# Four constants of an instruction schedule: an earlier start of attention, more dense work per block of keys, closer requests for weights

## The chip, the core and the metric

The kernel runs on one core of a Trainium2 chip. A core has TensorE (PE in the profile; its weight loads are the separate row PEld), VectorE (DVE), ScalarE (ACT), GpSimd (POOL) and SyncE (SP, which here issues every DMA). The metric is device time in microseconds (us); less is better. The kernel before took 713.68 us, the median of three runs that lie between 712.69 and 714.38 us. One more execution was profiled: it took 713.22 us, and the span from its first to its last instruction is 711.4 us, so 1.8 us lie outside the span.

## The reference, cut to what matters

The input x has 2048 rows of 512 numbers. The output mixes an attention block and an MLP row by row:

```
g = sigmoid((x * gate_w).sum(-1))
q, k, v = split(x @ wqkv)                  # 32 heads of 16
scores = q @ k.T / 4, kept where 0 <= query - key < 256
a = softmax(scores) @ v @ wo
b = gelu_tanh(x @ w1 + b1) @ w2 + b2       # 512 -> 1792 -> 512
out = g * a + (1 - g) * b
```

The kernel makes every dense product in three matmuls (high part times high part, high times low, low times high), so that two rounded factors together keep float32 accuracy.

## The kernel before, in words

**Dense work.** The rows are cut into four tiles of 512. One generator, `dense()` (L946), yields all dense work in pieces of three 128x512 matmuls (`mm3`, L124): first `qkv(t)` for the tiles 0 to 3 (eight q/k products and four v products each), then eight turns of `mlp`, then the output projection `final`. A turn of `mlp` is a tile with one half of the hidden columns: an **u stage** (28 pieces, the first MLP product; its results go through `gelu`, L746, three DVE and four ACT instructions per 128x512 block) and a **y stage** (28 pieces, the second product). There are thus eight u stages; the text numbers them u0 to u7 and the y stages y0 to y7.

**Attention.** Heads are taken four at a time in 8 groups, and the keys of a group in 16 blocks of 128: 128 steps of the loop at L976. A step holds four **maxima** (`att_max`, L539: matmul `sm` on PE, then a row maximum on DVE, L555), which run 12 steps ahead (`LEAD`), four **exponentials** (`att_exp`, L584: matmul `st` on PE, exponential on ACT, L617), and a mask of the block's edges on POOL (L611). After every fourth step `att_pvs` (L623) makes the product with v (`pv_sm` and `pv_st`, 64 to 96 small matmuls), evacuated by ACT (L660) and DVE (L663). After every fourth maximum step `att_rows` (L561) turns the maxima on DVE, and POOL copies them in eight casts into spare rows of `qs` (L577).

**What sets the order.** The program is written by hand, engine by engine: each engine executes its instructions in the order in which the Python code emits them, and waits for semaphores. The code keeps a clock of its own, `now`, in nanoseconds, which sets only the order and no time on the chip; `after(ns, fn)` emits something when that clock has moved on by `ns`. PE's order is written by `fill`, which emits dense pieces (counted at 681 ns each) until a budget is used up:

```
    fill(START - AHEAD)
    for c in (0, 1):
        load_ks(0, c)
    fill(AHEAD)
    for u in range(-LEAD, NU):
        step = STEP if u >= 0 else STEP0
        ... four times: one maximum, one exponential, fill(step / 4)
```

So `START` is the dense work ahead of the first maximum, `STEP0` (2750) the dense work in each of the 12 steps that hold maxima alone, and `STEP` the dense work in each of the 128 full steps. The dense work that the generator holds up to the output projection comes to 436.1 us by the code's count. In the y stages maxima and exponentials stand in pairs, in the u stages singly.

**Loads.** All DMAs go through SP's queue in order. `load_kd`, `load_qd`, `load_ks` and `load_qs` fetch the keys and queries of a group from DRAM. The two `load_ks` above stand `AHEAD` (9 us of dense work) before the first maximum; the first queries, `load_qd(0, 0)` and `load_qd(0, 1)`, are emitted at fixed pieces of `qkv(2)` (L447).

**Weights of the MLP.** `load` (L220) spaces the requests for w1, w2 and wo by at least `PACE` on the code's clock. A request that comes before `RAWS` lands in a spare half of a buffer of the exponentials (`half_pt`), and its low part is later subtracted on POOL (L201); one that comes after `RAWS` lands in one of two buffers `raw`, so that no more than two are under way, and its low part is subtracted on DVE (L201 too). The high part is always a copy on ACT (L197).

Of the kernel before, what the change touches and what calls it, by code (L numbers as in the profile page):

```python
# [32 lines left out]
def gated_mix(ctx: ExitStack, tc: tile.TileContext, x, wqkv, wo, w1, b1, w2, b2, gate_w, out):  # L33
# [100 lines left out]
    def after(ns, fn, *args):  # L134
        now[1] += 1
        heapq.heappush(todo, (now[0] + ns, now[1], fn, args))
# [20 lines left out]
    def half_pt(name):  # L157

        if not spare:
            v = sb.tile([128, 2, 2, 320], F32, tag="pt", bufs=PTS, name=name)  # L160
            v = v.rearrange("p h a b -> p h (a b)")
            spare.extend(v[:, h, 0:T] for h in (1, 0))
        return spare.pop()
# [4 lines left out]
    def load_raw(key, early=False):  # L168
# [6 lines left out]
        if early and kind == "v":  # L175
            if i == 0:
                raws["v"] = f32(sb.tile([128, NC, 2, T], F32R, tag="xt", bufs=1, name="raw_v"))
            raw = raws["v"][:, i, 0]
        elif early or now[0] < RAWS:
            raw = half_pt(f"raw_{kind}{i}")  # L180
# [39 lines left out]
    def load(key):  # L220

        paced[0] = max(now[0], paced[0] + PACE)
        after(paced[0] - now[0], load_now, key)
# [3 lines left out]
    def load_now(key):  # L227
        if now[0] >= RAWS:
            if slots[0] - slots[1] == 2:
                return after(500, load_now, key)  # L230
            slots[0] += 1
            after(LAND, split, key, nc.vector, True)
        else:
            after(LAND + 3000, split, key, nc.gpsimd)
        load_raw(key)
# [723 lines left out]
    def fill(ns):  # L959

        owed[0] += ns
        while owed[0] > 0:
            c = next(run)
            if c is None:
                owed[0] = -1e9
            else:
                owed[0] -= c
                tick(c)

    NU = NG * NKB  # L970
    NQ = NG * NT
# [5 lines that stand above are left out]
        m = u + LEAD  # L977
        gm, bm = divmod(m, NKB)
        step = STEP if u >= 0 else STEP0
        for i in range(4):  # L980
# [46 lines left out]
RB = 4  # L1027
NKB = S // 128
PTS = 7
RAWS = 152000.0  # L1030
PUT = 1200
LEAD = 12
QAT = 5
START = 105000.0
NORM = 6000
YSWAP = 3
GELU = (700, 1500, 3600, 4600, 6000, 7000)
XAT = 3
ORDER = 'mspf'
XOR = 1  # L1040
PACE = 4000.0
LAND = 7500.0
REACH = 2500.0
LAND0 = 11000.0
# [11 lines left out]
HELD = 2  # L1056
YAT = 5
YGAP = 2500
STEP = 2330.0
_TC = dict()  # L1060
_INS = ["A_x", "A_wqkv", "A_wo", "B_w1", "B_b1", "B_w2", "B_b2", "gate_w"]

# [17 lines left out]
```

## Time and profile before

| | |
|---|---|
| median of 3 runs | 713.68 us (712.69 to 714.38) |
| the profiled execution | 713.22 us, span 711.4 us |
| PE, PEld, DVE, ACT, POOL busy | 694.0, 596.5, 511.6, 419.6, 365.2 us |
| qkv(3), up to the first u matmul | ends 142.2 us after the span's start |
| u0 | 142.2 to 174.2 |
| u1 | 207.65 to 239.2 |
| u3 | 335.55 to 368.5 |
| u4 | 401.8 to 435.9 |
| output projection | 660.3 to 711.4 |

A row of the waits names the engine and line that waited, after the arrow who released it, and then the total in us, the number of waits and the longest. PE and PEld are one instruction stream: a weight load that waits holds the matmul behind it. A matmul's end is modelled, so that PE is shown as busy for a while after its last real step; a row of PEld is shown as idle from the end of its last load. A row of the stage table gives the stretch, its length, the busy time of each engine with the number of its instructions, the granted clock, the DMA engines' share and GB/s.

### The profile page before, as it was taken

To read this page: it belongs to the slowest core of one execution; us is meant where nothing else is said; L and a number is where in the kernel's file an instruction comes from. 1 tells how busy PE (TensorE), PEld (TensorE's weight loads), DVE (VectorE), ACT (ScalarE), POOL (GpSimd) and SP (SyncE) were. 2 spreads that over 40 slices of the span, in tenths; PEclk is the share of its full clock that TensorE was granted. 3 is DMA by queue.
4 is the path that set the end of the run, shared out by engine and by line. 5 is a ranking of instruction groups with operands and counts; after the bars stand their busy time and mean duration, and the time that the engine had idled before them with its cause. 6 is when DMAs were issued, how large, how long until landed. Compare 5 with 4: busy or idle time off the path is not lost.

```text
span 711.4 us, 17481 instructions
## 1 busy us (share of the span) xinstructions
PE 694.0 (98%) x6129; PEld 596.5 (84%) x6129; DVE 511.6 (72%) x1561; ACT 419.6 (59%) x972; POOL 365.2 (51%) x852
## 2 busy tenths in 40 slices
PE   9999999998999999999999999999999999999988
PEld 7888888886888888888888877888888888868876
DVE  4632425798769967986898799678968886875552
ACT  4434533378448845864795488458746853885451
POOL 5200001559756866776687578757865875620000
PEclk9999999999999999999999999999999999999999
DMA  9989798999996899999886989997899899477573
GB/s 315 355 256 364 261 373 279 266 295 246 245 249 155 211 274 249 217 279 277 220 194 176 240 234 247 252 260 174 185 246 239 194 260 270 124 217 230 188 243 119
DMA packets 179256, 172.09 MB, mean 242 GB/s; under 512 B 56673, under 2 KB 122977, under 8 KB 179169
## 3 DMA queue, kind: packets, MB, share of 16 engines
q1 hardware_dynamic: 179168, 170.97, 87.4%
q8 instruction: 49, 0.80, 0.5%
q14 instruction: 39, 0.31, 0.2%
HBM read 112.73 MB, written 62.39 MB: 246 GB/s over the span
## 4 chain that ended last, share of the span: by engine, by line
PE 77%; DVE 8%; ACT 5%; DMA 5%; POOL 3%; issue 1%; SPq 0%; DVEq 0%; ACTq 0%; POOLq 0%
PE sm L551 8%; PE pv_sm L639 7%; PE st L595 7%; PE y L127 6%; PE y L129 6%; PE y L128 6%; PE u L127 4%; PE qk L127 4%; PE u L129 4%; PE qk L129 4%; PE u L128 4%; PE qk L128 4%; DVE sm L555 3%; PE v L127 2%; PE v L129 2%; PE v L128 2%
## 5 line engine op out<-in xcount | busy, mean ns | idle before, releaser
L555 DVE CUSTOM_DVE_ANT_1 sm<-sm,mask 128x320 f32<-128x320 f32 (+4 forms) x512 | 232.8, 485 | 66.9 <-PE sm L551 61.8
L611 POOL TENSOR_SCALAR_AFFINE_SELECT pt<-pt 64x256 f32<-64x256 f32 (+1 forms) x538 | 215.1, 420 | 100.0 <-ACT pt L617 89.3
L617 ACT ACTIVATE pt<-st 128x320 f32<-128x320 f32 (+4 forms) x512 | 195.4, 422 | 116.7 <-PE st L595 115.9
L551 PE MATMUL sm<-kd,qd 96*128 96x320 f32 (+4 forms) x512 | 148.2, 303 | 5.0 <-DVE M L555 4.5
L595 PE MATMUL st<-qs,ks 128*128 128x320 f32 (+4 forms) x512 | 147.6, 299 | 1.1 <-ACT pt L617 1.0
L577 POOL CAST qs<-tt 4x256 fp32r<-4x256 f32 x256 | 121.5, 475 | 47.3 <-DVE tt L570 36.7
L551 PEld LDWEIGHTS sm<-kd,qd 96*128 96x128 f32 x512 | 96.8, 189 | 25.4 <-DVE M L555 11.4
L595 PEld LDWEIGHTS st<-qs,ks 128*128 128x128 f32 x512 | 97.5, 191 | 12.7 <-ACT pt L617 2.7
L127 PE MATMUL y<-w,h 128*128 128x512 f32 x224 | 85.1, 380 | 0.6 <-DVE sqh L756 0.6
L129 PE MATMUL y<-w,h 128*128 128x512 f32 x224 | 84.9, 379 | 0.0
L128 PE MATMUL y<-w,h 128*128 128x512 f32 x224 | 84.8, 379 | 0.0
L127 PE MATMUL u<-mx,w 128*128 128x512 f32 x196 | 77.1, 393 | 0.6 <-DVE sqh L756 0.6
L639 PE MATMUL pv_sm<-pt,vbuf 64*32 64x320 f32 (+4 forms) x1408 | 73.7, 346 | 1.0 <-POOL pt L611 1.0
L129 PE MATMUL u<-mx,w 128*128 128x512 f32 x196 | 74.3, 379 | 0.0
L128 PE MATMUL u<-mx,w 128*128 128x512 f32 x196 | 74.2, 378 | 0.0
L639 PE MATMUL pv_st<-pt,vbuf 64*32 64x320 f32 (+4 forms) x1408 | 73.5, 346 | 0.2 <-POOL pt L611 0.2
L555 DVE DVE_READ_ACCUMULATOR2_ANT M<- 128x1 f32 x512 | 71.5, 140 | 0.0
L639 PEld LDWEIGHTS pv_sm<-pt,vbuf 64*32 64x32 f32 x1408 | 49.3, 106 | 21.5 <-issue 2.0
L345 DVE TENSOR_TENSOR qke<-qk,qke 128x512 fp32r<-128x512 f32 x32 | 22.1, 690 | 43.2 <-ACT qke L342 28.2
L342 ACT ACTIVATE qke<-qk 128x512 fp32r<-128x512 f32 x32 | 19.1, 597 | 51.4 <-PE qk L129 30.0
L129 PEld LDWEIGHTS y<-w,h 128*128 128x128 f32 x224 | 42.2, 189 | 6.1
L660 ACT ACTIVATE nd<-pv_st 128x512 f32<-128x512 f32 x32 | 19.1, 597 | 45.2 <-PE pv_sm L639 39.4
(148 smaller groups left out, 1308.5 us busy)
## 6 DMA issues: line engine op xcount, KB each, us to landing
kd<-SK SPq DMA_DIRECT2D x32, 384.0 KB
qs<-SQ SPq DMA_DIRECT2D x64, 192.0 KB
mx<-XT SPq DMA_DIRECT2D x24, 512.0 KB
SQ<-qke SPq DMA_DIRECT2D x16, 512.0 KB
SK<-qke SPq DMA_DIRECT2D x16, 512.0 KB
ND<-nd SPq DMA_DIRECT2D x32, 256.0 KB
raw_w<-in_B_w_dram SPq DMA_DIRECT2D x28, 256.0 KB
qd<-SQ SPq DMA_DIRECT2D x32, 192.0 KB
```

The costliest lines, as they stand in the source:

```text
L127: nc.tensor.matmul(p, lh, rh, start=first, stop=False)
L128: nc.tensor.matmul(p, lh, rl, start=False, stop=False)
L129: nc.tensor.matmul(p, ll, rh, start=False, stop=last)
L342: nc.scalar.activation(halves(e[:, h]), p, AF.Copy)
L345: nc.vector.tensor_sub(halves(e[:, 1 - h]), p, halves(f32(e[:, h])))
L551: nc.tensor.matmul(v, qd[0:96, n, pr, 128 * j:128 * (j + 1)], two(kd[0:96, n, pr, k1 - w:k1]), start=True, stop=True)
L555: nc.vector.tensor_tensor_reduce(v, v, two(mask[:, 320 - w:320]), 1.0, -3e38, ALU.add, ALU.max, M[:, 2 * (b % RB) + hb, pr:pr + 1])
L577: nc.gpsimd.tensor_copy(dst, src.unsqueeze(1).broadcast_to([4, 2, RB, 32]))
L595: nc.tensor.matmul(pairs(p[:, :w]), ks[:, slot(g_, kb // NB), pr, at:at + 128], two(qs[:, pr, k0:k0 + w]), start=True, stop=True)
L611: nc.gpsimd.affine_select(out=v, in_=v, pattern=[[0, v.shape[1]], [1 - 2 * e, 64]], compare_op=ALU.is_ge, fill=0.0, base=-e, channel_multi ...
L617: nc.scalar.activation(halves(pt[:, hf, pr, :w]), sorted_(p[:, :w]), AF.Exp, scale=SCALE)
L639: nc.tensor.matmul(pv[r // 64][32 * i:32 * i + 32, q - c * T:e - c * T], vts[g_, b // NB][r:r + 64, v:v + 32], rhs(r), start=start, stop=s ...
```

## The change

Four constants change; no function does.

```
-RAWS = 152000.0
+RAWS = 146000.0
-START = 105000.0
+START = 97000.0
-PACE = 4000.0
+PACE = 3300.0
-STEP = 2330.0
+STEP = 2390.0
```

The first maximum is written 8 us of dense work earlier, within the last v product of `qkv(2)` in place of the third q/k product of `qkv(3)`. The first two loads of `ks` move with it. Each of the 128 full steps holds 2390 ns of dense work by the code's count in place of 2330, so the loop ends where it did: 97 + 12 x 2.75 + 128 x 2.39 = 435.92 us of dense work now, 105 + 12 x 2.75 + 128 x 2.33 = 436.24 before. Requests for weights may follow each other after 3300 ns, and the change of buffers and of the subtracting engine comes 6 us of the code's clock earlier.

**SP's queue around the first loads of attention.** `SQ` and `SK` are stores of q and k to DRAM, `ks` and `qd` the loads of keys and queries. Before:

```order
L349 DMA SQ_1_84<-qke_3_1052 128x2x512
L349 DMA SK_1_92<-qke_7_1076 128x2x512
L511 DMA qd<-SQ_0_79 48x8x128
L506 DMA qd<-SQ_0_79 48x7x128
L508 DMA qd<-SQ_0_79 48x2x64
```

Now:

```order
L349 DMA SQ_1_84<-qke_3_1052 128x2x512
L511 DMA ks<-SK_0_87 48x8x128
L506 DMA ks<-SK_0_87 48x7x128
L508 DMA ks<-SK_0_87 48x2x64
L511 DMA ks<-SK_0_89 48x8x128
L506 DMA ks<-SK_0_89 48x7x128
L508 DMA ks<-SK_0_89 48x2x64
L349 DMA SK_1_92<-qke_7_1076 128x2x512
L511 DMA qd<-SQ_0_79 48x8x128
L506 DMA qd<-SQ_0_79 48x7x128
L508 DMA qd<-SQ_0_79 48x2x64
```

Six loads of `ks` that stood behind both loads of `qd` now stand ahead of a store and of the first of them.

**PE at the beginning of u0** (`u` is the first MLP product, `sm` a maximum's matmul, `st` an exponential's). Before:

```order
L127 MATMUL u_0_1612<-xt_1009,w_0_1323 128x512
L128 MATMUL u_0_1612<-xt_1009,w_0_1323 128x512
L129 MATMUL u_0_1612<-xt_1009,w_0_1323 128x512
L551 MATMUL sm_9_3_1620<-kd,qd 128x320
L127 MATMUL u_0_1612<-xt_1009,w_0_1323 128x512
L128 MATMUL u_0_1612<-xt_1009,w_0_1323 128x512
L129 MATMUL u_0_1612<-xt_1009,w_0_1323 128x512
L551 MATMUL sm_9_2_1630<-kd,qd 128x320
```

Now:

```order
L127 MATMUL u_0_1665<-xt_1009,w_0_1346 128x512
L128 MATMUL u_0_1665<-xt_1009,w_0_1346 128x512
L129 MATMUL u_0_1665<-xt_1009,w_0_1346 128x512
L551 MATMUL sm_12_3_1677<-kd,qd 128x320
L595 MATMUL st_0_2_1680<-qs,ks 128x320
L127 MATMUL u_0_1665<-xt_1009,w_0_1346 128x512
L128 MATMUL u_0_1665<-xt_1009,w_0_1346 128x512
L129 MATMUL u_0_1665<-xt_1009,w_0_1346 128x512
L551 MATMUL sm_12_2_1690<-kd,qd 128x320
L595 MATMUL st_0_3_1692<-qs,ks 128x320
```

The stage began with maxima alone, at block 9 of the first group; it now begins with the first exponentials already beside them, at block 12. Counted in the two orders, u0 holds 31 maxima and 21 exponentials before and 32 of each now; the stages u1 to u7 hold 33, 32, 32, 33, 33, 32 and 16 maxima before and 32, 32, 32, 31, 31, 31 and 14 now. Of the low parts that fall into u0, POOL subtracts five before and four now, DVE three before and four now.

**DVE near the end** (`den` is the reciprocal of the last group's denominators, `ao` the output's last step on a block of 128 rows, `ot` and `num` the attention's result). Before:

```order
L912 SCALAR_TENSOR_TENSOR ao_10089<-a_2_0_10090,g,ao_10089 128x512
L740 TENSOR_TENSOR ot_3_10057<-ot_3_10057 128x512
L912 SCALAR_TENSOR_TENSOR ao_10089<-a_3_0_10111,g,ao_10089 128x512
L681 RECIPROCAL den_3_10106<-den_3_10106 128x32
L693 TENSOR_TENSOR num_3_10066<-num_3_10066,rb_3_10068 128x512
```

Now:

```order
L912 SCALAR_TENSOR_TENSOR ao_10089<-a_2_0_10090,g,ao_10089 128x512
L740 TENSOR_TENSOR ot_3_10054<-ot_3_10054 128x512
L681 RECIPROCAL den_3_10103<-den_3_10103 128x32
L912 SCALAR_TENSOR_TENSOR ao_10089<-a_3_0_10111,g,ao_10089 128x512
L693 TENSOR_TENSOR num_3_10067<-num_3_10067,rb_3_10069 128x512
```

The last reciprocal moves ahead of one output step. The reason is on PE: the last product with v stands behind two pieces of the output projection now and behind three before, because the dense work before the projection ends in another call of `fill`.

## The prediction

> **What bounds the kernel now.** I began with the page's totals.
>
> ```profile
> span 711.4 us, 17481 instructions
> PE 694.0 (98%) x6129; PEld 596.5 (84%) x6129; DVE 511.6 (72%) x1561; ACT 419.6 (59%) x972; POOL 365.2 (51%) x852
> ```
>
> PE is the bound, and the change gives it the same matmuls in another order. Time can therefore come or go only where PE waits. The waits of the weight loads show those in full, since a load that waits holds its matmul; here are the three largest with a named releaser.
>
> ```profile
> PEld sm L551 <- DVE M L555: 11.4, 24, 1.2
> PEld a L127 <- DVE ao L912: 3.4, 2, 2.8
> PEld st L595 <- ACT pt L617: 2.7, 5, 1.0
> ```
>
> The largest says that maxima are written faster than DVE reduces them: three buffers of `sm` are full, and PE stands. Next I cut the trace into stages by the first `u` and the first `y` matmul of each turn. These are u0, u1, u3 and u4: length, then PE, PEld, DVE, ACT and POOL busy.
>
> ```profile
> 142.20:174.17 31.97, 30.16 (x209) 24.24 (x208) 28.78 (x91) 25.02 (x52) 23.52 (x42) 1.00 1.00 254
> 207.65:239.20 31.55, 31.55 (x319) 27.62 (x318) 28.26 (x94) 25.23 (x59) 22.14 (x51) 1.00 0.80 171
> 335.55:368.49 32.94, 31.77 (x319) 27.42 (x317) 29.75 (x92) 26.84 (x61) 24.27 (x50) 1.00 0.91 218
> 401.84:435.88 34.04, 32.98 (x319) 27.46 (x318) 32.44 (x98) 27.70 (x63) 23.41 (x48) 1.00 0.93 231
> ```
>
> u1 carries a full load of attention and gelu and PE never idles. u0 executes a third fewer matmul records and is nevertheless longer. u3 and u4 have u1's matmuls and are 1.4 and 2.5 us longer; they also subtract weights on DVE. The granted clock is 1.00 in all four, so no throttle explains it. The weight loads' waits, first 142.2 to 180 us (u0 and the start of y0), then 335.55 to 372 (u3), 401.84 to 441 (u4) and 469.24 to 640 (u5 to u7):
>
> ```profile
> PEld sm L551 <- DVE M L555: 4.0, 7, 1.2
> PEld pv_sm L639 <- POOL pt L611: 1.2, 2, 0.9
> PEld pv_st L639 <- POOL pt L611: 0.5, 1, 0.5
> ...
> PEld pv_st L639 <- ACT pt L617: 1.1, 1, 1.1
> PEld sm L551 <- DVE M L555: 0.9, 3, 0.5
> ...
> PEld sm L551 <- DVE M L555: 3.6, 8, 0.7
> PEld sm L551 <- DVE nd L663: 0.7, 1, 0.7
> ...
> PEld st L595 <- ACT pt L617: 2.7, 5, 1.0
> PEld sm L551 <- DVE M L555: 1.5, 3, 0.8
> ```
>
> That is 5.7 us in u0, 2.0 in u3, 4.3 in u4 and 4.2 in u5 to u7. In u0 they fall late, when three engines are full at once:
>
> ```profile
> 157.00:162.00 5.00, 4.73 (x24) 3.65 (x23) 4.89 (x16) 4.97 (x13) 4.60 (x9) 1.00 1.13 234
> 162.00:167.00 5.00, 4.57 (x23) 3.59 (x23) 5.00 (x15) 4.97 (x13) 4.75 (x8) 1.00 0.39 121
> ```
>
> DVE, ACT and POOL are each busy 92 to 100% here while PE waits.
>
> [...] By PE's row the term for u0 below could not pass 1.8 us; by the loads' row it can reach 5.7.
>
> **The change part by part.** The sum is made against the profiled execution, 713.22 us, of which 1.8 us lie outside the span; the median is 0.46 us above it.
>
> *Fewer maxima per full step of dense work (STEP), and where it counts.* The prices, the second and third from u0, the others from u4:
>
> ```profile
> L555 DVE CUSTOM_DVE_ANT_1 sm<-sm,mask 128x320 f32<-128x320 f32 (+4 forms) x31 | 13.5, 455 | 0.8 <-PE st L595 0.6
> L197 ACT ACTIVATE w<-raw_w 128x512 fp32r<-128x512 f32 x8 | 5.1, 632 | 0.0
> L201 POOL TENSOR_TENSOR w<-raw_w,w 128x512 fp32r<-128x512 f32 x5 | 6.7, 1340 | 4.7 <-PE u L129 2.2 <-issue 1.6 <-POOL qs L577 0.8
> L555 DVE DVE_READ_ACCUMULATOR2_ANT M<- 128x1 f32 x32 | 4.4, 137 | 0.0
> L201 DVE TENSOR_TENSOR w<-raw_w,w 128x512 fp32r<-128x512 f32 x6 | 4.3, 722 | 0.0
> L663 DVE TENSOR_TENSOR nd<-nd,pv_sm 128x512 f32<-128x512 f32 x2 | 1.4, 681 | 0.4 <-ACT nd L660 0.4
> ```
>
> A maximum costs DVE 0.455 + 0.137 = 0.59 us. u4 goes from 33 to 31: 1.2 us less DVE work where DVE is 32.44 of 34.04 us busy. Between u3 (29.75 busy, 0.9 us of waits on DVE) and u4 (32.44 busy, 4.3 us), a microsecond of DVE work goes with 1.26 us of waits, so 1.2 us would give 1.5. I take **-1.2**, since part of the gain is handed to y4 (bounds 0 and -2.3, which is u3's level). u3 keeps its 32 maxima: 0. u5 goes from 33 to 31, u6 from 32 to 31, u7 from 16 to 14, five maxima or 3.0 us of DVE, but 2.7 of the 4.2 us there are waits for ACT, which loses only one to two exponentials a stage: **-0.8** (bounds 0 and -1.5, all of the waits on DVE). In the y stages one maximum more or less falls on idle DVE; u1 and u2 wait for nothing already: 0.
>
> *u0 (START, RAWS, PACE).* Before, its first 8 us held 10 maxima in the dense rhythm of the lead and gelu, then the exponentials joined. Now it holds 32 and 32 from the start, as u1 does. DVE: u1's 28.26 us, four subtractions (4 x 0.72 = 2.9), one less evacuation of a product with v (0.7), one of y less (about the same) and one maximum less (0.6): 29.2 us, below u3's 29.75, so at most u3's 0.9 us of waits on DVE in place of 4.0. But ACT: u1's 25.23 plus 8 copies at 0.63 is 30.3, less one evacuation 29.7 of some 32 us. And POOL: u1's 22.14 plus 4 x 1.34 is 27.5, where it has 23.5 now. Both will be fuller than in any u stage of this trace. The waits for POOL (1.7) stay at least; for ACT I add 1.4, between nothing and the 2.7 us that u5 to u7 show. After: 0.9 + 1.7 + 1.4 = 4.0 us in place of 5.7: **-1.7** (bounds: -4.8 if only u3's 0.9 us remain; +1.6 if the three engines' waits last as long again per us of full load, 5.7 x 32/25 with the exponentials present for 32 us in place of the 25 from 149 to 174).
>
> [...]
>
> *The first maxima.* They now stand where this matmul stands, and wait for `qd(0,0)`, whose three issues and the DMA engines' share around them are:
>
> ```profile
> 97.08 1.04 SPq L511 DMA_DIRECT2D qd<-SQ x1
> ...
> 99.40 0.60 SPq L508 DMA_DIRECT2D qd<-SQ x1
> ...
> 105.67 0.38 PE L127 MATMUL v<-v,qs 128*128 128x512 f32 x1
> ...
> 100.00:102.00 2.00, 2.00 (x11) 1.73 (x11) 0.00 (x0) 0.79 (x4) 0.00 (x0) 1.00 1.05 398
> 104.00:106.00 2.00, 2.00 (x11) 1.76 (x10) 1.16 (x2) 0.81 (x3) 0.15 (x1) 1.00 0.87 245
> ```
>
> The engines are full until about 104, so the queue is behind by some 4 us and `qd(0,0)` lands near 104; nobody wanted it then. Six loads of `ks` are now ahead of it:
>
> ```profile
> ks<-SK SPq DMA_DIRECT2D x32, 192.0 KB
> ks<-SK SPq DMA_DIRECT2D x32, 168.0 KB
> ks<-SK SPq DMA_DIRECT2D x32, 24.0 KB
> ```
>
> That is 2 x 384 KB, at 398 to 245 GB/s 2.0 to 3.2 us, which puts the landing at 106 to 107.2 against a PE that arrives at 105.67. Behind the waiting maximum stand all dense work of `qkv(3)`: **+1.0** (bounds 0, and +5.7: six issues at the 0.94 us that the three took each push the last issue from 100.0 to 105.6, and with the slowest landing that the chain shows for such a load,
>
> ```profile
> 539.46 5.70 DMA qd<-SQ
> ```
>
> it lands at 111.3). Later loads of queries stand 10 us and more ahead of their use: 0.
>
> *The end.* The reciprocal that waits for its DMA now holds back an output step one block earlier.
>
> ```profile
> 669.00 6.65 DMA ND<-nd
> 675.71 2.63 DMA den<-ND
> ```
>
> These two lead to the 3.4 us wait of the `a` matmuls. They start 0.65 us earlier (one piece, three matmuls of 0.216 us), and PE reaches the held-back block 2.6 us earlier, so it waits earlier, and then meets the next block's step about when it did before: 0 (bounds -0.7 and +0.7).
>
> *PACE otherwise.* With two buffers, later requests are spaced by the buffers; the copies keep at least 7.5 us of the code's clock for landing: 0.
>
> Sum: -1.2 - 0.8 - 1.7 + 1.0 = -2.7. The profiled execution would take 710.5 us; the median **711.0 us**, 0.4% less. The likeliest case's own range, half of each term's way to its bounds added in squares (1.8 down, 3.0 up), is 709.2 to 714.0.
>
> **The rivals.**
>
> *Nothing gained.* Three full engines at once are the cause in u0, and they stay full: its 5.7 us remain; u4 to u7 give 1.5, the first maxima cost 1.0: 713.2. For it: ACT and POOL in the two rows from 157 to 167. Against it: 4.0 of the 5.7 us are DVE's, and DVE's load falls below u3's.
>
> *Slower: the first maxima wait for their queries.* Place: the first `sm` on PE; price: up to 5.7 us; it decides once the wait passes the 3.7 us gained elsewhere by more than the measurement's uncertainty. With u0 giving 1.7 and u4 to u7 giving 2.0 the time is 713.68 + 5.7 - 3.7 = 715.7. For it: the full DMA engines at 100 us and a load that took 5.70 us. Against it: the bytes put ahead are only 2 to 3 us of transfer.
>
> [...]
>
> *More gained.* The overfull rhythm at the start of u0 caused the whole backlog; only u3's 2.0 us remain (-3.7), u4 falls to u3's level (-2.3), and `qd` is in time: -6.0 - 0.8 = -6.8, or 706.9. For it: u1 has no wait at all. Against it: u1 subtracts no weights.
>
> **How the numbers follow.** Forecast 0.50, nothing gained 0.22, slower 0.16, more gained 0.12. A change under 0.2% (1.4 us) is about what a measurement cannot tell from none. The forecast's own range passes 712.3, so 0.05 of it count as no change: faster 0.45 + 0.12 = 0.57, same 0.22 + 0.05 = 0.27, slower 0.16. The range 707.5 to 715.0 leaves out the far end of "more gained" (about 0.07) and of "slower" (about 0.1).
>
> **What would show it.** Right: in u0 the waits on DVE fall below 1 us and those on ACT or POOL take over; u4's fall from 4.3 to about 3; a first `sm` that waits for `qd` by about 1 us; `qkv(3)` longer by its 12 more maxima and two exponentials plus that wait. Wrong: u0's waits at 5.7 us or more, a `qd` wait of several us, or waits in u1 and u2, where there are none now.

## The result, and the profile after

The changed kernel is slower. Its median is 722.33 us (718.53 to 729.85, six runs) against 714.08 us (712.69 to 718.34, six runs) of the kernel before; the ratio is 1.0106 with a 95% interval of 1.0072 to 1.014. The forecast was 711.0 us, with a range of 707.5 to 715.0. The profiled execution of the changed kernel took 729.85 us, the longest of the six, and the ratio leaves it out: the other five took 718.53 to 726.78 us, so its stages show how time is lost, not how much is lost as a rule.

The totals of the page, and the waits of the weight loads over the whole span (three columns behind the colon: total in us, times, longest):

```profile
span 728.1 us, 17485 instructions
PE 699.8 (96%) x6129; PEld 603.0 (83%) x6129; DVE 512.3 (70%) x1562; ACT 421.2 (58%) x972; POOL 364.3 (50%) x851
```

```profile
PEld sm L551 <- DVE M L555: 12.0, 24, 2.2
PEld st L595 <- ACT pt L617: 7.6, 6, 3.8
PEld a L127 <- DVE ao L912: 6.4, 2, 5.8
...
PEld sm L551 <- DMA qd<-SQ: 1.9, 1, 1.9
```

The wait that was to shrink, 11.4 us before, is 12.0. The waits for `pt` rose from 2.7 to 7.6, those of the output projection from 3.4 to 6.4, and one wait for `qd` is new. The stages of before that the prediction does not show, `qkv(3)` and the output projection (stretch, length, busy us of PE, PEld, DVE, ACT and POOL, granted clock, share of the DMA engines, GB/s):

```profile
106.01:142.20 36.19, 36.19 (x184) 32.22 (x183) 24.75 (x97) 11.42 (x34) 12.40 (x21) 1.00 0.89 271
660.33:711.40 51.07, 45.24 (x303) 38.41 (x301) 23.49 (x38) 17.61 (x30) 0.00 (x0) 0.99 0.56 187
```

The same view after, cut at the same matmuls: `qkv(3)`, u0, u1, u4 and the output projection.

```profile
108.93:147.16 38.23, 38.12 (x196) 33.91 (x195) 30.59 (x121) 11.72 (x36) 14.31 (x26) 1.00 0.92 274
147.16:184.75 37.59, 32.85 (x221) 27.38 (x220) 28.37 (x87) 28.58 (x64) 28.23 (x56) 0.91 0.81 209
...
219.33:251.23 31.90, 31.66 (x317) 27.50 (x316) 26.20 (x87) 25.24 (x57) 22.27 (x53) 1.00 0.71 178
...
413.21:447.43 34.22, 32.34 (x316) 27.55 (x315) 31.38 (x95) 27.77 (x61) 23.09 (x50) 1.00 0.91 227
...
671.62:728.10 56.48, 47.73 (x303) 40.19 (x301) 23.69 (x38) 17.78 (x29) 0.00 (x0) 0.94 0.54 172
```

The span grew by 16.7 us. Up to the start of u1 it grew by 11.7 (207.65 to 219.33), from there to the projection by -0.4 (452.68 to 452.29), in the projection by 5.4. The loss sits at both ends, and in u0 and the projection the granted clock is below 1.00 (0.91 and 0.94). Three waits are the largest, and two smaller ones stand beside them.

**First place: the first maximum.** SP's timeline shows the first and last issue of `qd(0,0)`, and the windows show PE around it:

```profile
103.25 0.55 SPq L511 DMA_DIRECT2D qd<-SQ  x1
...
104.75 0.30 SPq L508 DMA_DIRECT2D qd<-SQ  x1
```

```profile
106.00:108.00 2.00, 0.60 (x3) 0.19 (x1) 0.30 (x1) 0.00 (x0) 0.00 (x0) 1.00 0.93 274
108.00:110.00 2.00, 1.88 (x10) 1.66 (x11) 1.09 (x6) 0.52 (x4) 0.16 (x1) 1.00 0.84 228
```

The last issue ends at 105.05 in place of 100.0 before, and PE works again just after 108. This is the 1.9 us wait above.

**Second place: a weight that lands late in u0.** From 147.16 to 190 us the weight loads wait once for 3.8 us, for an exponential. ACT's timeline shows why, and SP's shows the request behind it:

```profile
PEld st L595 <- ACT pt L617: 3.8, 1, 3.8
PEld sm L551 <- DVE M L555: 1.8, 5, 0.7
```

```profile
158.44 0.65 ACT L197 ACTIVATE w<-raw_w 128x512 fp32r<-128x512 f32 x1
163.43 0.63 ACT L197 ACTIVATE w<-raw_w 128x512 fp32r<-128x512 f32 x1 [4.34 <-DMA raw_w<-in_B_w_dram]
```

```profile
156.46 2.25 SPq L189 DMA_DIRECT2D raw_w<-in_B_w_dram  x1
```

ACT executes in the order of the code. It comes to the copy of a weight at 159.09 and stands there for 4.34 us, because SP put that weight's request out only from 156.46, 2.6 us earlier. The next exponentials stand behind the copy. The chain of waits shows what held the request back and how long it was under way; the first row below is SP's own wait, the other two are of the chain:

```profile
SPq L189 <- DMA ya<-in_B_b_dram: 2.4, 1, 2.4
```

```profile
148.60 7.85 DMA ya<-in_B_b_dram
...
156.46 6.95 DMA raw_w<-in_B_w_dram
```

SP stood 2.4 us until `ya`, an earlier load, had landed at 156.44, and the weight's load then took 6.95 us. Without SP's wait it would have landed near 161 (an estimate, 163.4 less 2.4), and ACT would still have stood some 1.9 us.

What follows costs nearly as much as the wait; in the windows PE's clock is the third number from the right:

```profile
160.00:162.00 2.00, 0.88 (x5) 0.61 (x4) 0.28 (x1) 0.00 (x0) 1.89 (x5) 1.00 0.87 271
162.00:164.00 2.00, 0.00 (x0) 0.00 (x0) 0.00 (x0) 0.57 (x2) 1.87 (x5) 1.00 0.57 169
164.00:166.00 2.00, 1.57 (x6) 0.97 (x6) 1.91 (x7) 1.97 (x6) 0.99 (x3) 0.89 0.09 18
166.00:168.00 2.00, 1.15 (x25) 0.78 (x32) 1.86 (x8) 2.00 (x5) 1.80 (x7) 0.50 0.82 234
...
170.00:172.00 2.00, 2.00 (x28) 1.34 (x13) 0.68 (x1) 0.60 (x1) 0.55 (x2) 0.50 1.12 222
172.00:174.00 2.00, 2.00 (x12) 1.87 (x11) 1.01 (x7) 1.38 (x3) 0.78 (x2) 0.90 1.20 250
```

After the pause the clock is halved: windows of 0.5 us read 0.50 from 166.0 to 172.0, 0.56 and 0.61 at the two edges, and 1.00 beyond them. A window of 2 us at clock c holds 2(1 - c)/0.5 us of half clock: 0.44, three times 2.0 (the window left out reads 0.50 too) and 0.40, together 6.8 us, in which PE does at most the work of 3.4.

**Third place: the end.** The store of the denominators on SP, and the chain of waits with the output projection's matmuls after it:

```profile
680.80 0.42 SPq L667 DMA_DIRECT2D ND<-nd  x1
```

```profile
684.62 7.24 DMA den<-ND
...
692.25 0.66 DVE ao L912
...
692.96 0.79 PE a L127
693.75 0.43 PE a L128
694.18 0.43 PE a L129
...
698.52 0.21 PE a L128
```

DVE stands at the reciprocal until `den` has landed, 7.24 us after its issue (2.63 us before), and the output step `ao` is now behind it. Most of that difference is not new, since the load was issued sooner after the store of the same denominators: from the issue of the store `ND` to the landing it is 9.3 us before (669.00 to 678.34) and 11.1 now (680.80 to 691.86). PE waits 5.8 us, and its next matmuls are 0.43 us apart until 698 and 0.21 to 0.22 after: half clock again.

**Two smaller waits.** Two more waits end with a landing. In y0 PE waits for keys near 202 us, and in the stage u6 (544.2 to 578.2 us) DVE stands at `num`, a step of the attention's result, until `rb` has landed; the maxima behind it are late, and PE waits 2.2 us:

```profile
PE st L595 <- DMA ks<-SK: 1.8, 1, 1.8
```

```profile
DVE num L693 <- DMA rb<-RD: 3.0, 1, 3.0
```

Neither is followed by half clock in this profile.

**How much of the loss is clock.** Each execution has its span and mean granted clock. Span times (1 - clock) is an estimate of what half clock cost it. It is on the high side where PE still waits while the clock is halved, as at the end for some 1.8 us before 692.96 (0.8 us in the window from 690 to 692, whose clock is 0.80, and 0.96 behind it). Means over the executions that the comparisons use:

| kernel | executions | time | of it by half clock | rest |
|---|---|---|---|---|
| before (beside the experiments) | 79 | 714.3 | 0.9 | 713.5 |
| the change | 5 | 722.0 | 4.5 | 717.5 |

Of 7.7 us lost, some 3.6 are clock by this estimate and some 4.1 are the rest.

### The profile page after: what moved, and what is told of

Same layout as the page of the kernel before. It is cut to its first block, busy times and chain, and to the rows that moved or that the text cites. A ratio compares the mean times of both kernels' runs of the same rounds, so it can differ in the third digit from the quotient of the medians.

```text
span 728.1 us, 17485 instructions
## 1 busy us (share of the span) xinstructions
PE 699.8 (96%) x6129; PEld 603.0 (83%) x6129; DVE 512.3 (70%) x1562; ACT 421.2 (58%) x972; POOL 364.3 (50%) x851
## 4 chain that ended last, share of the span: by engine, by line
PE 59%; DMA 8%; DVE 7%; ACT 5%; SPq 2%; issue 2%; DVEq 0%; ACTq 0%
PE sm L551 8%; PE st L595 7%; PE pv_sm L639 6%; PE y L127 6%; PE y L129 6%; PE y L128 6%; PE u L127 4%; PE u L129 4%; PE u L128 4%; DVE sm L555 2%; PE pv_st L639 2%; PE a L127 2%; PE a L128 2%; PE a L129 2%; ACT pt L617 1%
## 5 line engine op out<-in xcount | busy, mean ns | idle before, releaser
L611 POOL TENSOR_SCALAR_AFFINE_SELECT pt<-pt 64x256 f32<-64x256 f32 (+1 forms) x538 | 217.9, 425 | 102.1 <-ACT pt L617 91.5
L577 POOL CAST qs<-tt 4x256 fp32r<-4x256 f32 x256 | 119.4, 467 | 70.3 <-DVE tt L570 53.2
L639 PE MATMUL pv_sm<-pt,vbuf 64*32 64x320 f32 (+4 forms) x1408 | 75.8, 352 | 0.9 <-DVE nm L567 0.8
L639 PE MATMUL pv_st<-pt,vbuf 64*32 64x320 f32 (+4 forms) x1408 | 75.0, 352 | 0.0
L639 PEld LDWEIGHTS pv_sm<-pt,vbuf 64*32 64x32 f32 x1408 | 52.5, 108 | 19.9 <-issue 2.0
L639 PEld LDWEIGHTS pv_st<-pt,vbuf 64*32 64x32 f32 x1408 | 47.9, 107 | 0.2
```

The lines of the kernel that those rows point to most:

```text
L577: nc.gpsimd.tensor_copy(dst, src.unsqueeze(1).broadcast_to([4, 2, RB, 32]))
L611: nc.gpsimd.affine_select(out=v, in_=v, pattern=[[0, v.shape[1]], [1 - 2 * e, 64]], compare_op=ALU.is_ge, fill=0.0, base=-e, channel_multi ...
L639: nc.tensor.matmul(pv[r // 64][32 * i:32 * i + 32, q - c * T:e - c * T], vts[g_, b // NB][r:r + 64, v:v + 32], rhs(r), start=start, stop=s ...
```

## The experiments

Three groups: take away the three waits, singly and together; make one part of the change alone, or undo one; and put them together anew. Times are medians, ratios go to the kernel before on the same chip. "v2 to u1" is the stretch from the first v product of `qkv(2)` to the first matmul of u1 in the profile, the one that holds the first two places and the wait for keys: 112.9 us before, 123.8 us after. The 8 us that START gives up are some three steps of attention (8/2.39); they stand in this stretch now and are absent later.

**1. More time for the weights of u0.** Against the changed kernel, in `load_now`:

```
-            after(LAND, split, key, nc.vector, True)
+            after(LAND + (3000 if now[0] < 200e3 else 0), split, key, nc.vector, True)
```

The copy of a weight that lands in `raw` is emitted 10.5 us after its request, as for the buffers of the exponentials, in place of 7.5.

> The changed kernel, with one edit: in u0 the high-part copies of the weights that land in the two raw buffers are placed 3 us later on ACT (10.5 us of the code's clock for landing in place of 7.5). Theory A (a weight copy at the head of ACT's queue waits for its load, the exponentials behind it hold PE, and PE's long wait halves the granted clock for 6.8 us): the 4.3 us wait of ACT for the load falls under 1 us, no wait of a weight load of st over 1 us in u0, no stretch of half clock near 165 us, u0 back from 37.6 to 31 to 33 us, the time 4 to 7 us below the changed kernel's (about 715 to 717). Rival B (in u0 ACT, DVE and POOL are full with 32 maxima, 32 exponentials and the weights, wherever the copies stand): u0 stays above 36 us and the time within 1.5 us of the changed kernel's.

Measured: 721.04 us, ratio 1.0076 (1.0041 to 1.011). The stage came out as expected, the time did not. In u0 ACT waits 0.28 us for that weight, u0 takes 32.4 us in place of 37.6, v2 to u1 119.0. The other two waits stay, 1.9 and 4.2 us, each followed by half clock (the mean clock of the execution is 0.995). The windows behind the first:

```profile
108.00:110.00 2.00, 1.85 (x7) 1.54 (x8) 1.14 (x6) 0.35 (x3) 0.15 (x1) 0.80 0.76 208
110.00:112.00 2.00, 2.00 (x7) 1.64 (x7) 1.01 (x5) 0.43 (x3) 0.00 (x0) 0.50 0.65 207
112.00:114.00 2.00, 2.00 (x10) 1.75 (x9) 0.73 (x5) 0.00 (x0) 0.00 (x0) 0.85 0.52 155
```

That is 0.8 + 2.0 + 0.6 = 3.4 us at half clock after a wait of 1.9 us. So the late weight is the cause of u0's length, but its cure alone gives back only a part that the intervals do not separate from nothing. In this profile the wait in u6 is longer, 3.2 us in place of 2.2, after DVE has stood 4.1 us for `rb`.

**2. The queries ahead of the keys again.** Against the changed kernel; the `load_ks` then stand 1 us of dense work ahead of the first maximum:

```
-AHEAD = 9e3
+AHEAD = 1e3
```

> The changed kernel, with one edit: the first two loads of ks are written 1 us of dense work ahead of the first maximum in place of 9, so that they stand behind the first loads of queries again. Theory A: the first maximum's wait for qd (1.9 us) falls under 0.5 us and qkv(3) begins 1.5 to 2 us earlier; u0 and the end keep their waits; the time 1 to 2.5 us below the changed kernel's. Rival: qd lands late because the queue is full anyway, and the wait stays at 1 us or more.

Measured: 722.23 us, ratio 1.0106 (1.0063 to 1.0149); the gain of 1 to 2.5 us was not there. The wait for `qd` is gone and `qkv(3)` starts at 107.2 in place of 108.9. But y0 starts at 184.5, as after (184.8). The gain went into u0, which is the row

```profile
145.60:184.51 38.91, 33.74 (x221) 27.36 (x220) 27.92 (x88) 28.66 (x64) 27.96 (x56) 0.91 0.84 223
```

where ACT waits longer for weights than the 4.3 us after:

```profile
ACT w L197 <- DMA raw_w<-in_B_w_dram: 6.6, 2, 4.3
```

In this profile the stall that ends with a landing took back what was gained ahead of it, so this cure shows no gain.

**3. The last product with v one piece later.** Against the changed kernel, so that the reciprocal stands behind the output step again:

```
-HELD = 2
+HELD = 3
```

> The changed kernel, with one edit: the last product with v stands behind three pieces of the output projection, as before the change, which puts the last reciprocal behind the output step of block 3 on DVE again. Theory A (the reciprocal waits for its DMA and holds back an output step that PE needs one block earlier): the a matmuls' wait falls from 6.4 us to 3.5 or less, no half clock near 691 us, the output projection back from 56.5 to 51 to 52.5 us, the time 3 to 5.5 us below the changed kernel's. Rival (the DMA of the denominators is merely slower in that run, 7.2 us in place of 2.6, and the place of the reciprocal does not matter): the wait varies with the DMA, and the end stays at 54 us or more.

Measured: 722.39 us, ratio 1.0112 (1.0057 to 1.0168). The projection takes 51.3 us with no half clock behind its wait, against 56.5 after and 51.07 before. But a wait of 3.1 us is still there, the first two places are as bad as after (v2 to u1 124.3), and the time shows no gain, where 3 to 5.5 us were expected. The wait in u6 is 3.4 us here, and this time 3.4 us of half clock follow it (the mean clock of the execution is 0.990). The profile is again the longest of its executions (727.18 us of four).

**4. All three together.**

> The changed kernel with the three edits together: copies 3 us later in u0, the first ks loads behind the first queries, three pieces ahead of the last product with v. Theory A (these three waits are all that the change costs, and its relief of DVE is real): 708 to 712 us, below the kernel before. Rival B (the change itself brings nothing: waits in u0 stay): 713 to 718 us.

Measured: 713.97 us, ratio 0.999 (0.9966 to 1.0015). The whole loss is gone, but the time lies in the range of the second reading (713 to 718), not below the kernel before. u0 and u4:

```profile
145.50:177.30 31.80, 29.86 (x221) 26.00 (x220) 27.01 (x86) 27.77 (x63) 28.57 (x54) 1.00 1.03 265
...
404.91:438.11 33.20, 32.26 (x316) 27.52 (x315) 31.26 (x95) 27.77 (x61) 23.92 (x50) 1.00 0.94 237
```

```profile
PEld sm L551 <- DVE M L555: 10.8, 24, 1.2
PEld st L595 <- ACT pt L617: 3.4, 5, 1.4
PEld a L127 <- DVE ao L912: 3.3, 3, 2.3
```

u0 executes 32 maxima and 32 exponentials in 31.8 us, where before 31 and 21 took 31.97. ACT still stands 2.3 us in front of a weight in u0, but no exponential that PE wants is late by more than 1.4 us. No wait of the weight loads passes 2.3 us, and the clock is 1.00. The three edits together take the whole loss away. They do not touch the wait in u6, which is short in this profile too (DVE stands 1.1 us for `rb`); in the profile of experiment 7 it is shorter still (0.7 us) and the loss stays, so that wait is not the main part of it. What the change was to bring is then seen alone: the profiled span is 1.0 us shorter than before (710.4 against 711.4), the median no different.

**5. PACE alone, on the kernel before.**

```
-PACE = 4000.0
+PACE = 3300.0
```

> The kernel before with PACE 3300 alone: requests for weights closer together, nothing else. Theory A (what hurts in u0 is a copy on ACT that is placed 7.5 us after its request, where loads are late; here only the last two of the first weights have 7.5 us, the others 10.5): no wait of ACT for a weight of over 1.5 us in u0, no half clock, 712 to 716 us, the same as before. Theory P (closer requests crowd the DMA queue, and any schedule with them suffers): ACT waits 3 us or more for a weight in u0 and the time is 718 us or more.

Measured: 714.45 us, ratio 1.001 (0.9978 to 1.0043). ACT waits for no weight and u0 takes 31.8 us. In its profile, with mean clock 0.997, the end waits 3.1 us, with 3.4 us of half clock behind it, so the end can cost something without the change too, and the expectation of no half clock missed there.

**6. The change without PACE.**

```
-PACE = 3300.0
+PACE = 4000.0
```

> The changed kernel with PACE back at 4000. Theory A: the third w2 block is now the first with the short allowance of 7.5 us, asked for while the DMA queue is as full as before, so ACT still waits 2 us or more for a weight and u0 stays at 35 us or more; the time within 2.5 us of the changed kernel's (719 to 724). Theory P: requests 4 us apart relieve the queue, ACT's wait falls under 1 us, u0 to 31 to 33 us, the time to 715 to 718.

Measured: 719.9 us, ratio 1.0073 (1.004 to 1.0107). The reading by which ACT would go on waiting 2 us or more, with u0 at 35 us or more, missed. ACT waits

```profile
ACT w L197 <- DMA raw_w<-in_B_w_dram: 0.8, 1, 0.8
```

and u0 takes 33.7 us. The stall is smaller, but it is not gone: DVE's subtraction waits 1.1 us for that copy, PE waits 2.2 us for the maxima behind it, and half clock follows:

```profile
162.00:164.00 2.00, 2.00 (x7) 1.69 (x6) 2.00 (x9) 1.45 (x3) 1.90 (x4) 0.52 0.90 259
164.00:166.00 2.00, 2.00 (x9) 1.71 (x7) 1.86 (x9) 1.96 (x5) 1.82 (x7) 0.63 1.09 265
```

So the closer requests make the late weight later; the other edits suffice for a late one. The wait for `qd` stays, at 2.3 us.

**7. The change without RAWS.**

```
-RAWS = 146000.0
+RAWS = 152000.0
```

> The changed kernel with RAWS back at 152000: two more blocks of w2 land in halves of the exponentials' buffers, get 10.5 us for landing, and are subtracted on POOL. Theory A: as with the later copies, ACT's wait for a weight falls under 1 us and no half clock follows in u0; u0 31 to 34 us (POOL has two subtractions more, 2.7 us, so waits for POOL may grow); the waits for qd and at the end stay; 715 to 720 us. Theory P: ACT waits as before, 720 us or more.

Measured: 721.22 us, ratio 1.0081 (1.0046 to 1.0116). ACT's wait is 1.1 us and u0 takes 33.1 us, so RAWS has a part in the late weight too. But the wait for `qd` is 2.8 us and that at the end 4.6 us, each with 3.4 us of half clock behind it (the mean clock of the execution is 0.995), and the time hardly moves: it is 1.2 us above the range of the reading that the waits come nearest to.

**8. The kernel before with the keys ahead of the queries.**

```
-AHEAD = 9e3
+AHEAD = 17e3
```

> The kernel before with the first two loads of ks 17 us of dense work ahead of the first maximum in place of 9: they stand ahead of the first loads of queries as in the changed kernel, but the first maximum keeps its old place. Theory A (the wait for qd is made of two things, a load pushed back and a maximum pulled forward): no wait of a maximum for qd, 712.5 to 715.5 us, the same as before. Rival: the queue itself suffers from the loads at that place (stores of q and k late, later waits), 716 us or more.

Measured: 713.99 us, ratio 1.0018 (0.9986 to 1.0051), with no wait for `qd`. The earlier keys do no harm by themselves; they do when the first maximum is earlier too.

**9. START and STEP alone.** Against the changed kernel, RAWS and PACE as before:

```
-RAWS = 146000.0
-PACE = 3300.0
+RAWS = 152000.0
+PACE = 4000.0
```

> Edit: START and STEP as changed, RAWS 152000 and PACE 4000 as before, so the change of attention alone. Theory A (three separate waits; the late weight of u0 needs RAWS and PACE both): ACT waits for a raw weight for under 0.5 us and u0 takes 31.8 to 33.0 us, but the first maximum still waits 1.9 to 2.8 us for qd and the end still waits 3 to 6 us, each sometimes with 3.4 us of half clock: 717 to 720.5 us, ratio 1.004 to 1.009. Rival P (the weight requests are the whole cause): 712 to 714.5 us. Rival S (full load in u0 is the cause whatever the weights do): u0 at 35 us or more, 720 us or more.

Measured: 720.63 us, ratio 1.0071 (1.0034 to 1.0108): the separate-waits reading, 0.1 us above its range of time. u0 takes 31.5 us and ACT waits for no weight, though u0 is as full of attention as after. So it is the weight, not the fullness, that stretched u0. The wait for `qd` is 2.9 us, and this time the clock stays up:

```profile
106.00:108.00 2.00, 0.00 (x1) 0.00 (x0) 0.00 (x0) 0.00 (x0) 0.00 (x0) 1.00 0.99 269
108.00:110.00 2.00, 1.49 (x7) 1.31 (x8) 1.11 (x6) 0.12 (x1) 0.15 (x1) 1.00 0.66 191
110.00:112.00 2.00, 2.00 (x14) 1.79 (x12) 1.16 (x6) 0.67 (x4) 0.00 (x0) 1.00 0.73 210
```

The profiled execution, with clock 1.000, took 716.41 us; the others, at 0.993 to 0.998, took 715.09 to 724.87.

**10. RAWS alone, on the kernel before.**

```
-RAWS = 152000.0
+RAWS = 146000.0
```

> Edit: the kernel before with RAWS 146000 alone. Theory A: with the exponentials joining late and requests 4000 apart ACT waits under 1 us for a weight, no first maximum waits for qd, u0 at 31.5 to 33 us: 713 to 715.5 us. Rival R (a weight moved early out of the exponentials' buffers is enough by itself to make ACT wait): ACT waits 2 us or more for a raw weight, u0 34 us or more, 716 us or more.

Measured: 713.68 us, ratio 0.9989 (0.996 to 1.0018), v2 to u1 111.7 us, no wait of ACT for a weight in u0. Neither RAWS nor PACE by itself does harm without the earlier start; the two together without it were not run.

**11. The three cures, PACE as before.** Experiment 4 with `PACE = 4000.0`.

> Edit: the change with the three waits removed (weights asked for earlier before 200 us, ks before qd taken away, the held-back step one more) and PACE 4000 as before. Theory A (with the waits gone, PACE is worth nothing, only the lighter steps are): 712 to 714.5 us, ratio 0.997 to 1.001, the same as with PACE 3300 (713.97). Rival P2 (closer requests add DMA traffic where engines are full and cost the relief): 0.5 to 1.5 us less than with PACE 3300, 712 to 713.3 us. Rival P3 (closer requests are what makes u4 to u7 shorter): 715 us or more.

Measured: 714.43 us, ratio 1.0004 (0.9979 to 1.0028), against 713.97 and 0.999 with 3300: no difference, as the first reading has it. Closer requests are worth nothing measurable. In the profile PE waits 1.3 and 1.1 us for a weight in y0, and v2 to u1 is 117.5 us against 115.4 in experiment 4, a difference that the medians do not confirm.

**12. START and STEP with the cures for `qd` and the end.** Experiment 9 with `AHEAD = 1e3` and `HELD = 3`.

> Edit: START and STEP as changed, RAWS and PACE as before, AHEAD 1e3 and HELD 3: the change of attention alone with the waits for qd and at the end removed. Theory A: no wait over 2 us for qd or for a weight, u0 at 31.8 to 33 us, end wait 2 to 4 us: 712.5 to 715 us, ratio 0.998 to 1.002. Rival G (the lighter steps gain what was predicted, 2.7 us or more, and the weight edits were what ate it): 710 to 711.5 us, ratio 0.996 or less. Rival S (a full u0 costs by itself): 716 us or more with u0 at 34 us or more.

Measured: 716.85 us, ratio 1.0022 (0.9991 to 1.0054). The waits are as expected (no wait for `qd`, 0.4 us for a weight in u0, 2.4 us at the end; u0 takes 31.5 us), the median is 1.9 us above the range given: a miss in size, and not separated from before. The profile has two things that the expectation left out: DVE stands 2.5 us for `rb` in u6 and PE 1.9 us behind it, and 3.4 us of half clock follow the wait at the end (the mean clock of the execution is 0.998). No version tried is measurably faster than the kernel before.

The estimate of clock and rest, as above, for the kernels that matter:

| kernel | executions | time | by half clock | rest |
|---|---|---|---|---|
| more time for weights (1) | 9 | 720.6 | 4.0 | 716.6 |
| all three cures (4) | 10 | 713.7 | 0.3 | 713.4 |
| without PACE (6) | 6 | 719.9 | 2.3 | 717.6 |
| START and STEP (9) | 9 | 720.3 | 3.2 | 717.1 |
| with two cures (12) | 11 | 715.6 | 1.2 | 714.3 |

From 9 to 12 the cures for `qd` and the end give 4.8 us, 2.0 of it clock; with the longest execution of 12 counted too (724.45 us) it is 4.0. From the change (722.0) to 9, without the late weight, it is 1.7 us, which the intervals do not resolve. How the 7.7 us divide among the three places is therefore not settled to better than this; that the three edits take back the whole is shown by experiment 4.

## Why the prediction was wrong

**"PACE otherwise: 0" failed.** The step said that the copies keep at least 7.5 us of the code's clock for landing. They do, but that clock puts only the order; what counts is when SP gets to the request and how long the load is under way. SP itself stood 2.4 us for `ya`, so the request left at 156.46; it took 6.95 us, and the copy had come to the head of ACT at 159.09. Three edits meet in that place: RAWS puts a weight that had 10.5 us onto the path with 7.5, PACE brings requests closer, START fills ACT behind it. In experiments 5, 6, 7, 9 and 10, which lack one or two of them, ACT's wait in u0 is at most 1.1 us, though 0.8 us still cost PE 2.2 us and half clock in 6. START missing alone was not run, so its part is argued.

**u0, -1.7: the mechanism was right, the stage was read for load alone.** In u0 the waits for DVE did fall: 1.8 us in place of 4.0 for `sm`; those for POOL, which the step kept at 1.7, were 0.3. With the late weight cured, a fully loaded u0 takes 30.8 to 32.4 us (experiments 1, 4, 9, 11, 12), about as long as the partly loaded one did (31.97). But the +1.4 us that the step gave to ACT was a price of ACT being busy. ACT lost 4.3 us standing in front of a DMA, which no row of busy time shows.

**The first maxima, +1.0: right in place, too small.** Measured 1.9, 1.9, 2.6, 2.3, 2.8 and 2.9 us in the six profiles that have the wait (the change, experiments 1, 3, 6, 7, 9), inside the bounds of 0 and 5.7. The landing was put at 106 to 107.2; it was about 108. The bytes ahead were priced by their share of the bandwidth; the issues also moved, from 100.0 to 105.05, which only the upper bound had (105.6). That the six loads put ahead hold `qd` back, on which the +1.0 and the rival "Slower" rest, was the author's assumption, and no run shows it by itself: what the runs show is the wait of 1.9 to 2.9 us, and in experiment 2 no wait once the six loads stood behind `qd`, where the moved issues alone would do that too.

**"The end: 0" failed.** The step let PE wait earlier and then meet the next block's step when it did before. It took the way of the denominators from before. From the issue of the store to the reciprocal that is 9.5 us before and 7.9 to 9.7 in the other profiles with the old order, but 10.2 to 11.2 in all six with the changed order, and PE, which by the step itself comes 2.6 us earlier to the block behind it, waits for that longer way. In the other profiles with the changed order the wait at the end is 1.2 us (6) to 4.6 us (7), with the old order 1.8 (8) to 3.1 us (3, 5). The two overlap, so the +3.0 us of the changed kernel's profile is an upper case. Why the way is longer was not isolated.

**What had no term at all: the clock.** "The granted clock is 1.00 in all four, so no throttle explains it" was true of that one execution. It was taken to hold for what the change adds, too, and "Time can therefore come or go only where PE waits" left the clock out. Each wait was priced at its own length, but here waits of 1.9 to 5.8 us of PE brought 3.4 or 6.8 us at half clock, that is up to 1.7 or 3.4 us more. By the table that is some 3.6 of the 7.7 us.

**The lighter steps, -1.2 and -0.8: small.** With the waits cured, u4 takes 33.2 us in place of 34.0. Its waits for `sm` on DVE, 3.6 us before, are 0.9 (404.9 to 442 us of experiment 4), but a part has moved to the next matmul that needs DVE:

```profile
PEld pv_sm L639 <- DVE M L555: 1.3, 2, 1.1
PEld sm L551 <- DVE M L555: 0.9, 1, 0.9
```

The whole kernel gains 1.0 us in its profile and 0.1% in its ratio, whose interval holds no change, against the -3.7 us of the three terms of relief. "Nothing gained" (0.22) was the better forecast for that part. Which stage takes the difference back was not isolated.

**The rivals.** "Slower" was given 0.16 and one place, the first maxima, at 715.7 us. The side and the place were right; it lacked the other two places, and the clock.

## What to carry to other kernels

An edit that starts work sooner must be followed into every load whose lead it shortens: take the time at which the DMA queue really issues the request, and look for what stands behind the consumer on its in-order engine (here the exponentials behind the copy at which ACT stood for 4.34 us). Price a pause of the bound engine with what its clock loses after it, here up to 1.7 or 3.4 us more after waits of 1.9 to 5.8 us, and look at several executions' clocks before setting that to zero. And when several stalls end with landings, curing one may show nothing; cure them together, then put them back one at a time.

## What the runs showed of the hardware

PE's granted clock fell from 1.00 to 0.50 after short pauses, for 3.4 us (experiments 1, 6) or 6.8 us (u0 and the end after); in the projection of the changed kernel matmuls are then 0.43 us apart in place of 0.21 to 0.22. Half clock followed waits of 1.9 us (experiment 1), 2.2 (6), 2.8 (7), 3.8 (u0 after) and 5.8 us (the end after), but not the 2.8 us at the end of the kernel before, the 2.9 us of experiment 9 or the 3.2 us in u6 of experiment 1. Its length does not go by that of the wait alone: 6.8 us followed the 3.8 us in u0 after, and 3.4 us followed 4.6 us at the end of experiment 7. So in these profiles a wait of 2 to 3 us cost its length in one and up to 1.7 us more in another. Of the 79 executions of the kernel before, 41 have a mean clock of 1.000 and take 713.2 us in the mean; the other 38 have less and take 715.5.
